# Attention in front of two mixture layers: rotation two pairs ahead, the first head rotated by VectorE, a half-width rotation table, another order at the last pair

## The chip, the core and the metric

One core of a Trainium2 chip runs one program: attention over 16 heads, then two mixture-of-experts layers. The metric is device time in microseconds (us) from start to end of the program; lower is better. The engines named below are TensorE (PE in the rows; its weight loads are PEld), VectorE (DVE), ScalarE (ACT), GpSimd (POOL) and SyncE (SP), which issues most of the DMAs. Each engine works through its own instructions in program order.

## The reference, cut to what matters

Only the attention is touched by the change. Its result, reshaped to `x`, feeds the two mixture layers.

```python
batch, n_heads, seq, head_dim = (2, 8, 576, 64)
def rotate(x):
    x1, x2 = (x[..., :half], x[..., half:])
    return np.concatenate([x1 * cos - x2 * sin, x1 * sin + x2 * cos], axis=-1)
q_rot, k_rot = (rotate(q), rotate(k))
scores = scale * np.matmul(q_rot, k_rot.transpose(0, 1, 3, 2))
scores = scores - np.max(scores, axis=-1, keepdims=True)
attn = np.exp(scores)
attn = attn / (np.sum(attn, axis=-1, keepdims=True) + 1e-09)
return np.matmul(attn, v).astype(np.float32)
...
x = np.ascontiguousarray(attn_out.transpose(0, 2, 1, 3)).reshape(B * S, H * D)
x = _moe_ref(x=x, **moe_kwargs)
return _moe2_ref(x=x, **moe2_kwargs)
```

## The kernel before, in words

`attention` works on 16 heads `g` (2 batches of 8), in 8 pairs `P`; the first head of a pair has `h = 0`, the second `h = 1`. All is in float32. The order of the work is written out by hand: for each head a list of calls with a number each (`at(t, f, ...)`) is sorted by the number and run. The integer part of a number is the tile of 128 score rows (five per head) beside which the call stands; `SC` holds the numbers of the calls that recur.

For a pair, `load_q` and `load_k` bring the raw heads to `rawq` and `rawk` (one buffer each). `rot` turns them: two products with the sine part of the table into `t2`, a product with the cosine part in place, and a sum into `t1` (`t1q`, `t1k`: two buffers each, one pair in each). `t1q` holds each value twice, side by side; the second copy is written by a second sum for pair 0, and by two small DMAs on SyncE's queue (one per head) for the others. From pair 1 on, all of `rot` is GpSimd's. `prepare(P + 1, n)`, called in the first head of pair P, rotates the next pair and then calls `preload`, which loads the raw data of the pair after that; SyncE issues all these DMAs in program order and waits where a buffer is still in use.

`tq(g)` transposes the rotated q and k of head `g` on TensorE (15 small matmuls against `ident`, 10 that read `t1q` and 5 that read `t1k`), and ScalarE and VectorE copy the result out to `qk`. It stands at 1.5 of the head before. `score(g, i)` multiplies a tile, VectorE takes the negative maximum (`negmax`), ScalarE the exponential with its row sum. `te` transposes the exponentials (one half is copied out by ScalarE, the other, `te_b`, by VectorE), and `pv` multiplies them with v one pair later. `rcp` (4.4 of the second head) inverts the row sums on VectorE, and GpSimd spreads the result over a tile `rcp`. `rbc` (0.5 of the next first head) transposes that tile on TensorE, and `norm` scales the output `xn`. `xsplit` writes `xn` as a rounded part `xH` (ScalarE) and a rest `xL` (GpSimd).

`warm(n)` issues n matmuls on a zero tile `wb` with no use of the result: 8 and 6 at the start, 3 behind the first `tq`, and 3 in each of the five steps of head 0.

Behind head 15 a last list (`g == NG`) finishes the last two pairs and begins the first mixture layer: `m1.step` with k = 0 (12 matmuls and two copies), then k = 1, and the rest in `m1.rest`. `m1.wconv(s, part)` splits a block of weights into a rounded part (ScalarE, or VectorE with `True` as last argument) and a rest (GpSimd, line 607). Everything behind that is not touched.

Of the kernel before, what the change touches and what calls it, by code (L numbers as in the profile page):

```python
# [1133 lines left out]

WC = dict(a=2.5, b=4.6, c=1.9, d=2.5)


def attention(tc, nc, ps, pss, lp, q, k, v, rope, ident, xH, xL, m1):
    with ExitStack() as st:
# [46 lines left out]
        def load_v(P):  # L1186
            t = vs[P % 2]
            for h in range(2):
# [35 lines left out]

        def rot(P, n, hs=(0, 1), e1=G, e2=G):
            x, tb = raw[n], tab[n]
# [11 lines left out]

            e1.tensor_tensor(t2[:, o, :, 0:32], x[:, o, :, 32:64], table(64, 96), op=OP.mult)
            e1.tensor_tensor(t2[:, o, :, 32:64], x[:, o, :, 0:32], table(96, 128), op=OP.mult)  # L1240
            e2.tensor_tensor(x[:, o], x[:, o], table(0, 64), op=OP.mult)  # L1241
            e2.tensor_tensor(t1, x[:, o], t2[:, o], op=OP.add)  # L1242
# [137 lines left out]
        for g in range(NG + 1):  # L1380
# [6 lines left out]
            if g < NG:  # L1387
                for i in range(5):
# [6 lines left out]
                    if g == 0:  # L1395
                        at(i + 0.4, warm, WARM[3])
# [22 lines left out]
            if m1 and g == NG - 1:  # L1419
                at(WC["a"], m1.wconv, 0, 0, True)  # L1420
                at(WC["b"], m1.wconv, 0, 1, True)
                at(4.5, m1.wload, 2)
            if g == NG:
                at(0.0, norm, P - 2, 1)
                at(0.0, xsplit, P - 2)
                at(0.1, rbc, P - 1)
                at(0.2, pv, P - 1, 0, 0, 5)
                at(0.3, norm, P - 1, 0)
                if m1:
                    at(0.4, m1.step)  # L1430
                    at(0.5, m1.wconv, 1, 0)
                at(0.6, pv, P - 1, 1, 0, 5)
                if m1:
                    at(0.7, m1.wconv, 1, 1)
                    at(0.7, m1.gate_w)
                    at(0.7, m1.wload, 3)
# [71 lines left out]
```

## Time and profile before

| | us |
|---|---|
| median of 3 runs | 1195.23 (1194.79 to 1198.83) |
| the profiled execution: its time | 1194.06 |
| the profiled execution: its span | 1192.1 |
| TensorE busy | 1129.7 (95% of the span) |
| VectorE, ScalarE, GpSimd busy | 769.9, 373.2, 448.4 |

The attention is the first 220 us or so of the span; the rest is the two mixture layers. The span is what the rows cover; the time is 2 us longer. Busy time of an engine is summed over its instructions; a row of the trace's timeline gives when an instruction or a merged run of like instructions began, how long it was busy, how many there were, and in brackets how long the engine had been idle before it and who released it.

### The profile page before, as it was taken

What the parts mean: (1) busy time and instruction counts of PE and PEld (TensorE: products, weight loads), DVE (VectorE), ACT (ScalarE), POOL (GpSimd) and SP (SyncE); (2) the same over time, 40 slices, a digit from 0 to 9 for tenths busy, and PEclk for the clock granted to TensorE, in tenths of its full rate; (3) what the DMA queues carried; (4) which work ended last, traced back from release to release, by engine and by line L of the source; (5) the groups of instructions that cost most, each with busy time, mean ns of one, the idle gap of its engine ahead of it and who ended that gap; (6) DMA issues with size and microseconds to landing.
All of it is one profiled execution on the core that took longest, in us unless ns stands there. A gap on an engine that the chain in (4) does not pass through costs nothing.

```text
span 1192.1 us, 20710 instructions
## 1 busy us (share of the span) xinstructions
PE 1129.7 (95%) x8147; PEld 975.2 (82%) x8147; DVE 769.9 (65%) x1721; ACT 373.2 (31%) x851; POOL 448.4 (38%) x432
## 2 busy tenths in 40 slices
PE   6877777999999999999999999999999999999997
PEld 3555545799888988888898888888989887899997
DVE  5655556146467777777777777666668888889200
ACT  3655555322332323232323232332232120222222
POOL 6345551521643544344434443544320000364121
PEclk7988888999999999999999999999999999999999
DMA  4121113310022232324222322121113003878830
GB/s 110 37 52 42 42 42 93 100 48 1 31 68 71 90 114 89 89 71 131 82 89 86 118 89 90 47 60 36 36 60 118 27 1 122 279 270 285 270 102 20
DMA packets 105297, 107.57 MB, mean 90 GB/s; under 512 B 35440, under 2 KB 68336, under 8 KB 105072
## 3 DMA queue, kind: packets, MB, share of 16 engines
q1 hardware_dynamic: 102864, 100.80, 27.1%
q0 software_dynamic: 2048, 4.72, 1.3%
q8 instruction: 64, 1.05, 0.4%
q10 hardware_dynamic: 288, 0.72, 0.2%
q14 instruction: 33, 0.27, 0.1%
HBM read 99.21 MB, written 4.72 MB: 87 GB/s over the span
## 4 chain that ended last, share of the span: by engine, by line
PE 81%; POOL 7%; issue 5%; DVE 3%; DMA 3%; ACT 1%; SPq 0%; POOLq 0%; DVEq 0%; ACTq 0%
PE Y L927 24%; PE T L865 22%; PE Y L701 8%; PE T L682 8%; PE Y L422 5%; PE Y L432 4%; PE PV L1319 2%; PE S L1283 1%; PE T L1260 1%; DMA t1q<-t1q 1%; POOL rawk L1241 1%; PE T L241 1%; POOL t1k L1242 1%; POOL rawq L1241 1%; POOL t1q L1242 1%
## 5 line engine op out<-in xcount | busy, mean ns | idle before, releaser
L929 DVE SCALAR_TENSOR_TENSOR acc<-Y,pw,acc 128x512 f32<-128x512 f32 x216 | 158.3, 743 | 1.5 <-PE Y L927 0.4
L865 PE MATMUL T<-xH,wa 128*128 128x256 f32 (+1 forms) x576 | 137.4, 294 | 0.8 <-ACT v L885 0.8
L865 PEld LDWEIGHTS T<-big,wb 128*128 128x128 f32 x864 | 125.8, 188 | 10.5 <-DVE v L878 1.4
L878 DVE TENSOR_TENSOR v<-T,v 128x256 f32<-128x256 f32 (+1 forms) x240 | 108.3, 451 | 38.2 <-PE T L865 35.3
L865 PE MATMUL T<-big,wb 128*128 128x256 f32 (+1 forms) x864 | 132.8, 296 | 0.0
L865 PEld LDWEIGHTS T<-xH,wa 128*128 128x128 f32 x576 | 100.0, 188 | 8.3 <-ACT v L885 2.5
L682 PE MATMUL T<-xH,wa 128*128 128x384 f32 x336 | 92.9, 337 | 0.0
L1285 DVE TENSOR_REDUCE negmax<-S 128x1 f32<-128x576 f32 (+1 forms) x80 | 60.2, 753 | 48.0 <-PE S L1283 47.9
L774 POOL TENSOR_TENSOR wa<-wraw,wa 128x512 fp32r<-128x512 f32 (+1 forms) x48 | 48.9, 1019 | 104.9 <-ACT wa L773 104.9
L865 PE MATMUL T<-xL,wa 128*128 128x256 f32 (+1 forms) x288 | 84.5, 293 | 0.0
L872 DVE SCALAR_TENSOR_TENSOR hlB<-v,hhB 128x320 fp32r<-128x320 f32 x72 | 56.9, 790 | 38.8 <-ACT hhB L871 38.8
L871 ACT ACTIVATE hhB<-v 128x320 fp32r<-128x320 f32 x72 | 34.0, 472 | 136.0 <-DVE v L878 136.0
L871 ACT ACTIVATE hhA<-v 128x256 fp32r<-128x256 f32 x72 | 30.1, 418 | 148.2 <-DVE v L878 148.2
L927 PE MATMUL Y<-wa,hhB 128*128 128x512 f32 x240 | 75.3, 396 | 0.0
L927 PE MATMUL Y<-wb,hhB 128*128 128x512 f32 x240 | 75.2, 395 | 0.0
L872 DVE SCALAR_TENSOR_TENSOR hlA<-v,hhA 128x256 fp32r<-128x256 f32 x72 | 50.6, 702 | 35.3 <-ACT hhA L871 35.3
L1000 DVE SCALAR_TENSOR_TENSOR fr<-fr,fc 128x512 f32<-128x512 f32 x64 | 52.5, 820 | 32.0 <-DMA fr<-in_moe_w 32.0
L793 POOL TENSOR_TENSOR wb<-wraw,wb 128x512 fp32r<-128x512 f32 x24 | 30.6, 1296 | 102.0 <-ACT wb L792 102.0
L701 PE MATMUL Y<-wb,hh 128*128 128x512 f32 x216 | 68.3, 397 | 0.0
L793 POOL TENSOR_TENSOR wa<-wraw,wa 128x512 fp32r<-128x512 f32 x24 | 30.6, 1292 | 99.8 <-ACT wa L792 99.8
L1283 PE MATMUL S<-qk 64*128 64x288 f32 x320 | 63.9, 477 | 1.5 <-ACT big L1288 1.4
L682 PEld LDWEIGHTS T<-xH,wa 128*128 128x128 f32 x336 | 61.3, 188 | 2.9 <-issue 0.9
(286 smaller groups left out, 2667.5 us busy)
## 6 DMA issues: line engine op xcount, KB each, us to landing
wraw<-in_moe_w SPq DMA_DIRECT2D x52, 512.0 KB, 5.4
fr<-in_moe_w SPq DMA_DIRECT2D x64, 256.0 KB, 4.2
wraw<-in_moe_w SPq DMA_DIRECT2D x48, 256.0 KB, 2.8
big<-in_moe_w SPq DMA_DIRECT2D x20, 512.0 KB, 4.6
wa<-in_moe_w SPq DMA_DIRECT2D x18, 512.0 KB, 3.9
wb<-in_moe_w SPq DMA_DIRECT2D x14, 512.0 KB, 4.2
fc<-in_moe_w_gate SPq DMA_DIRECT2D x9, 256.0 KB
ysc<-acc SPq DMA_DIRECT2D x9, 256.0 KB, 2.1
```

Of the source, the lines that this page charges most:

```text
L422: nc.tensor.matmul(Z["ph"][:, f % 2], d["wa"][kt // 2][:, kt % 2, f * 128:(f + 1) * 128], Z["xg", p][:, kt], start=(kt == 0), stop=(kt == ...
L682: nc.tensor.matmul(p[:, :CH], w[:, wi, kt, (fb % 2) * 128:(fb % 2) * 128 + 128], x[:, kt, o], start=(n == 0), stop=(n == 11))
L701: nc.tensor.matmul(self.Y[c][t], a[:, o], w[:, wi, fb % 2], start=(fb == 0 and n == 0), stop=(fb == FB - 1 and n == 2))
L793: G.tensor_tensor(d["W"][:, 1, h], r[:, 2 + h], d["W"][:, 0, h].bitcast(F32), op=OP.subtract)
L865: nc.tensor.matmul(bank[:, 0:n], d[t][:, ww, b, r * 128:(r + 1) * 128], x(xw, r), start=(first and i == 0), stop=(i == 5), skip_group_chec ...
L871: A.activation(HH[:, f, o], src, AF.Relu)
L872: V.scalar_tensor_tensor(HL[:, f, o], src, 0.0, HH[:, f, o].bitcast(F32), op0=OP.max, op1=OP.subtract)
L878: V.tensor_tensor(o, bank[:, 0:n], x, op=OP.add)
L927: nc.tensor.matmul(y, h[:, f, o], w[:, ww, f], start=(f == 0 and z == 0), stop=(f == 1 and z == 2))
L929: V.scalar_tensor_tensor(self.acc[:, t], y, self.pw[:, t, e:e + 1], self.acc[:, t], op0=OP.mult, op1=OP.add)
L1283: T.matmul(p[:, a, :288], QK[g][o, i * 128:(i + 1) * 128], QK[g][o, 640:928], start=True, stop=True)
L1285: V.tensor_reduce(m[0:n], p[0:n, :, :288], axis=AX.XY, op=OP.max, negate=True)
```

## The change

- Rotation two pairs ahead: `prepare(P + 2, ...)` stands in the second head of pair P, where `prepare(P + 1, ...)` stood in the first. So the raw data of pair P + 3 are loaded then. Pair 1 is prepared apart: its k on GpSimd before the loop, its q on VectorE in head 0, at 2.6 and 3.6.
- Pair 0: head 0 is rotated by VectorE as before, with the `wb` memset between k and q; the second copy of `t1q` is written by ScalarE. `tq(0)` follows at once, then head 1's k on VectorE (before: GpSimd) and its q on GpSimd.
- Table: the host sends 64 columns (cosine, sine) in place of 128; ScalarE writes the full table from them with six activations. The first q and its tail are issued on ScalarE's queue.
- `warm`: 6, 2, and 2 in each step of head 0, in place of 8, 6, 3 and 3.
- `xsplit`: the rounded part `xH` is GpSimd's but for the last pair. `rcp` of the last pair is spread by ScalarE.
- Last pair: the weight splits stand at 0.6, 1.6 and 3.6 of head 15 (before 2.5 and 4.6, and one behind it); `m1.step` with k = 0 stands ahead of `rbc` and `pv`, k = 1 between the two `pv`.

```diff
-WC = dict(a=2.5, b=4.6, c=1.9, d=2.5)
+WC = (0.6, 1.6, 3.6)
...
+        tcs = pone.tile([128, 11, 64], F32, name="tcs")
         load_k(nc.sync, 0, (0,), False)
-        A.dma_start(tab["k"], rope[:, 5:11])
-        load_q(nc.sync, 0, (0,), False)
-        A.dma_start(tab["q"], rope[:, 0:5])
+        A.dma_start(tcs[:, 5:11], rope[:, 5:11])
+        load_q(A, 0, (0,), False)
+        A.dma_start(tcs[:, 0:5], rope[:, 0:5])
...
+        for n, o in (("k", slice(5, 11)), ("q", slice(0, 5))):
+            A.activation(tab[n][:, :, 64:96], tcs[:, o, 32:64], AF.Copy, scale=-1.0)
+            A.activation(tab[n][:, :, 96:128], tcs[:, o, 32:64], AF.Copy)
+            A.activation(tab[n][:, :, 0:64].rearrange("p j (u c) -> p j u c", u=2),
+                         tcs[:, o, 0:32].unsqueeze(2).to_broadcast([128, SL[n], 2, 32]), AF.Copy)
...
             if U == 2:
-                dup = T1[n, P][:, o, :, 1]
-                if P == 0:
-                    e2.tensor_tensor(dup, x[:, o], t2[:, o], op=OP.add)
+                d = T1[n, P][:, o, :, 1]
+                if dup is None:
+                    for i in range(len(hs)):
+                        nc.sync.dma_start(d[:, i], t1[:, i])
                 else:
-                    for i in hs:
-                        nc.sync.dma_start(dup[:, i], t1[:, i])
+                    dup(d, t1)
...
-            A.activation(xH[:, pr, o], XN[P], AF.Copy)
+            if P < NP - 1:
+                G.tensor_copy(xH[:, pr, o], XN[P])
+            else:
+                A.activation(xH[:, pr, o], XN[P], AF.Copy)
...
+        def copy(d, x):
+            A.activation(d, x, AF.Copy)
+
+        rot(0, "k", (0,), V)
+        V.memset(wb, 0.0)
+        rot(0, "q", (0,), V, copy)
         warm(WARM[0])
-        rot(0, "k", (0,), V, V)
-        rot(0, "q", (0,), V, V)
-        warm(WARM[1])
-        rot(0, "k", (1,), G, G)
-        rot(0, "q", (1,), G, G)
+        tq(0)
+        rot(0, "k", (1,), V)
+        rot(0, "q", (1,), G, copy)
         preload(1, "k")
         preload(1, "q")
-        tq(0)
-        warm(WARM[2])
+        warm(WARM[1])
+        rot(1, "k")
+        preload(2, "k")
...
-                if h == 0:
-                    at(SC["rk"], prepare, P + 1, "k")
-                    at(SC["rq"], prepare, P + 1, "q")
-                else:
+                if g == 0:
+                    at(2.6, rot, 1, "q", (0,), V)
+                    at(3.6, rot, 1, "q", (1,), V)
+                    at(3.6, preload, 2, "q")
+                if h == 1:
+                    at(SC["rk"], prepare, P + 2, "k")
+                    at(SC["rq"], prepare, P + 2, "q")
                     at(SC["rcp"], rcp, P)
...
-                at(WC["a"], m1.wconv, 0, 0, True)
-                at(WC["b"], m1.wconv, 0, 1, True)
-                at(4.5, m1.wload, 2)
+                for t, w in enumerate(((0, 0, True), (0, 1, True), (1, 0))):
+                    at(WC[t], m1.wconv, *w)
+                at(1.6, m1.wload, 2)
...
-WARM = (8, 6, 3, 3)
+WARM = (6, 2, 2)
```

Three places show what the new order does. The first is GpSimd's list from the rotation of pair 1 to the first spread of inverted sums (`rcp`). Before, pair 1's k and q (`t1k_244`, `t1q_323`) stand ahead of it, and pair 2's begin behind it:

```order
L1239 TENSOR_TENSOR t2k_244<-rawk_96,tabk_98 128x12x32
L1240 TENSOR_TENSOR t2k_244<-rawk_96,tabk_98 128x12x32
L1241 TENSOR_TENSOR rawk_96<-rawk_96,tabk_98 128x768
L1242 TENSOR_TENSOR t1k_243<-rawk_96,t2k_244 128x768
L1239 TENSOR_TENSOR t2q_324<-rawq_95,tabq_97 128x10x32
L1240 TENSOR_TENSOR t2q_324<-rawq_95,tabq_97 128x10x32
L1241 TENSOR_TENSOR rawq_95<-rawq_95,tabq_97 128x640
L1242 TENSOR_TENSOR t1q_323<-rawq_95,t2q_324 128x10x64
L1327 COPY rcp_492<-den_489 128x640
L1239 TENSOR_TENSOR t2k_531<-rawk_96,tabk_98 128x12x32
```

Of the change, the end of pair 1's k (`t1k_203`), then all of pair 2 (`t1k_392`, `t1q_464`), the same `rcp`, and pair 3's k behind it:

```order
L1247 TENSOR_TENSOR t1k_203<-rawk_96,t2k_204 128x768
L1244 TENSOR_TENSOR t2k_393<-rawk_96,tabk_98 128x12x32
L1245 TENSOR_TENSOR t2k_393<-rawk_96,tabk_98 128x12x32
L1246 TENSOR_TENSOR rawk_96<-rawk_96,tabk_98 128x768
L1247 TENSOR_TENSOR t1k_392<-rawk_96,t2k_393 128x768
L1244 TENSOR_TENSOR t2q_465<-rawq_95,tabq_97 128x10x32
L1245 TENSOR_TENSOR t2q_465<-rawq_95,tabq_97 128x10x32
L1246 TENSOR_TENSOR rawq_95<-rawq_95,tabq_97 128x640
L1247 TENSOR_TENSOR t1q_464<-rawq_95,t2q_465 128x10x64
L1334 COPY rcp_511<-den_508 128x640
L1244 TENSOR_TENSOR t2k_677<-rawk_96,tabk_98 128x12x32
```

So the `rcp` of pair P, which stood behind the rotation of pair P + 1, stands behind that of pair P + 2.

The second place is VectorE's opening, of the change, from the last memset to the second rotation of k (the same list before has the `wb` memset ahead of the first row, a second sum of line 1246 ahead of the `qk` copy, and `negmax` right behind that copy):

```order
L1216 MEMSET big_100 128x64 x3
L1244 TENSOR_TENSOR t2k<-rawk,tabk 128x6x32
L1245 TENSOR_TENSOR t2k<-rawk,tabk 128x6x32
L1246 TENSOR_TENSOR rawk<-rawk,tabk 128x384
L1247 TENSOR_TENSOR t1k<-rawk,t2k 128x384
L1382 MEMSET wb 128x256
L1244 TENSOR_TENSOR t2q<-rawq,tabq 128x5x32
L1245 TENSOR_TENSOR t2q<-rawq,tabq 128x5x32
L1246 TENSOR_TENSOR rawq<-rawq,tabq 128x320
L1247 TENSOR_TENSOR t1q<-rawq,t2q 128x5x64
L1278 COPY qk<-T 128x7x64
L1244 TENSOR_TENSOR t2k<-rawk,tabk 128x6x32
```

The last row is the first of four that rotate k of head 1; they have come between the copy of head 0's transposes and its first maximum.

The third place is ScalarE's list from head 15's end to the second step of the mixture layer. Before, with `hh` of `m1.step` k = 0 and k = 1 behind the copies `rs` of `rbc`:

```order
L1336 ACTIVATE rs_2566<-T_2567 128x4x64
L1338 ACTIVATE rs_2566<-T_2567 128x64
L690 ACTIVATE hh_2611<-T_2598 128x384
L606 ACTIVATE wa_2615<-wraw_2406 128x1024
L606 ACTIVATE wb_2629<-wraw_2406 128x1024
L538 ACTIVATE gg_2409<-g1_2404 128x4x8
L1349 ACTIVATE xH_71<-xn_2592 128x576
L690 ACTIVATE hh_2653<-T_2640 128x384
```

And of the change:

```order
L606 ACTIVATE wa_2543<-wraw_2402 128x1024
L1336 ACTIVATE rcp_2556<-den_2553 128x640
L690 ACTIVATE hh_2582<-T_2569 128x384
L606 ACTIVATE wb_2586<-wraw_2402 128x1024
L1345 ACTIVATE rs_2589<-T_2590 128x4x64
L1347 ACTIVATE rs_2589<-T_2590 128x64
L690 ACTIVATE hh_2630<-T_2617 128x384
L538 ACTIVATE gg_2405<-g1_2400 128x4x8
```

The first `hh` and both weight splits now stand ahead of `rs`, and `rcp` is in this list.

## Rows read from the trace of the kernel before

**Rows 1.** Page, span in 40 equal slices: granted clock in tenths.

```profile
PEclk7988888999999999999999999999999999999999
```

**Rows 2.** Waits, 0 to 240 us: total us, times, longest.

```profile
PE T L1260 <- DMA t1q<-t1q: 30.1, 6, 5.5
```

**Rows 3.** Timeline of TensorE: transposes of rotated q that begin `tq`.

```profile
32.90 0.53 PE L1260 MATMUL T<-ident,t1q 64*128 64x64 f32 x9 [0.50 <-ACT pt L1306]
...
41.16 0.52 PE L1260 MATMUL T<-ident,t1q 64*128 64x64 f32 x9 [0.47 <-ACT pt L1306]
...
52.34 0.53 PE L1260 MATMUL T<-ident,t1q 64*128 64x64 f32 x10 [2.71 <-DMA t1q<-t1q]
...
63.51 0.85 PE L1260 MATMUL T<-ident,t1q 64*128 64x64 f32 x10 [0.27 <-ACT rs L1338]
...
77.79 0.80 PE L1260 MATMUL T<-ident,t1q 64*128 64x64 f32 x10 [5.47 <-DMA t1q<-t1q]
...
193.80 0.85 PE L1260 MATMUL T<-ident,t1q 64*128 64x64 f32 x10 [0.27 <-ACT rs L1338]
```

**Rows 4.** Windows: busy us by engine, then granted clock, DMA share, GB/s.

```profile
82.80:84.10 1.30, 1.30 (x8) 0.57 (x6) 0.00 (x0) 0.00 (x0) 0.00 (x0) 0.60 0.00 0
...
88.00:114.00 26.00, 19.76 (x220) 13.38 (x222) 14.55 (x30) 13.98 (x35) 12.37 (x10) 0.87 0.23 53
```

**Rows 5.** Timeline of GpSimd and SyncE's queue, pair 2 to 3.

```profile
63.14 1.41 POOL L1350 TENSOR_TENSOR xL<-xn,xH 128x576 fp32r<-128x576 f32 x1 [1.89 <-ACT xH L1349]
...
64.51 1.00 POOL L1239 TENSOR_TENSOR t2k<-rawk,tabk 128x384 f32<-128x384 f32 x1
...
73.58 1.53 POOL L1242 TENSOR_TENSOR t1q<-rawq,t2q 128x640 f32<-128x640 f32 x1
...
75.14 1.33 SPq L1249 DMA_DIRECT2D t1q<-t1q  x2
...
87.12 0.72 POOL L1327 COPY rcp<-den 128x640 f32<-128x640 f32 x1 [12.01 <-DVE den L1325]
```

**Rows 6.** Lines by shape, 30 to 200 us: busy, mean ns, idle before.

```profile
L1306 ACT ACTIVATE pt<-T 128x320 f32<-128x320 f32 x56 | 24.4, 436 | 42.5 <-PE T L1260 42.5
...
L1349 ACT ACTIVATE xH<-xn 128x576 fp32r<-128x576 f32 x6 | 4.0, 673 | 0.0
```

**Rows 7.** Timeline of the opening: VectorE and TensorE.

```profile
6.79 0.36 DVE L1239 TENSOR_TENSOR t2k<-rawk,tabk 128x192 f32<-128x192 f32 x1 [5.14 <-DMA rawk<-in_k]
...
8.79 0.70 DVE L1239 TENSOR_TENSOR t2q<-rawq,tabq 128x160 f32<-128x160 f32 x1
...
12.45 0.80 DVE L1246 TENSOR_TENSOR t1q<-rawq,t2q 128x320 f32<-128x320 f32 x1
...
13.40 0.80 PE L1260 MATMUL T<-ident,t1q 64*128 64x64 f32 x10 [6.84 <-DVE t1q L1246]
...
17.18 0.76 DVE L1285 TENSOR_REDUCE negmax<-S 128x1 f32<-128x576 f32 x1 [2.11 <-PE S L1283]
```

**Rows 8.** Timeline of the opening: SyncE's queue and GpSimd, pair 1.

```profile
9.78 2.58 SPq L1175 DMA_DIRECT2D rawk<-in_k  x4
...
15.69 0.99 POOL L1239 TENSOR_TENSOR t2k<-rawk,tabk 128x384 f32<-128x384 f32 x1
...
21.34 0.86 POOL L1239 TENSOR_TENSOR t2q<-rawq,tabq 128x320 f32<-128x320 f32 x1
```

**Rows 9.** Timeline at the last pair: VectorE and TensorE.

```profile
205.00 0.68 DVE L604 CAST wa<-wraw 128x1024 fp32r<-128x1024 f32 x1
...
209.62 0.52 PE L1260 MATMUL T<-ident,rcp 64*128 64x64 f32 x9 [2.01 <-POOL rcp L1327]
```

**Rows 10.** Chain that ended last, at the last pair: start, us, what.

```profile
210.14 4.26 PE PV L1319 x20
...
216.68 2.58 PE PV L1319 x20
...
223.59 2.08 PE T L682 x12
```

More of the change, by code (lines that the diff above doesn't have):

```diff
@@ L1204, in attention @@
         load_k(nc.sync, 0, ())
-        load_q(nc.sync, 0, ())
+        load_q(A, 0, ())
         load_k(nc.sync, 0, (1,), False)
@@ L1213, in attention @@
         wb = one.tile([128, 512], BF, name="wb")
-        V.memset(wb, 0.0)
         for i in range(NE):
             V.memset(eb[i][:, 576:640], 0.0)
+        for n, o in (("k", slice(5, 11)), ("q", slice(0, 5))):
[3 more added lines that the diff above has]
+                         tcs[:, o, 0:32].unsqueeze(2).to_broadcast([128, SL[n], 2, 32]), AF.Copy)
         def warm(n):
@@ L1223, in attention, with rot @@
         T1 = {}
-        def rot(P, n, hs=(0, 1), e1=G, e2=G):
+        def rot(P, n, hs=(0, 1), e=G, dup=None):
             x, tb = raw[n], tab[n]
@@ L1237, in table @@
                 return tb[:, :, lo:hi].unsqueeze(1).to_broadcast([128, len(hs), J, hi - lo])
[L1239 to L1242, printed above, removed]
+            e.tensor_tensor(t2[:, o, :, 0:32], x[:, o, :, 32:64], table(64, 96), op=OP.mult)
+            e.tensor_tensor(t2[:, o, :, 32:64], x[:, o, :, 0:32], table(96, 128), op=OP.mult)
+            e.tensor_tensor(x[:, o], x[:, o], table(0, 64), op=OP.mult)
+            e.tensor_tensor(t1, x[:, o], t2[:, o], op=OP.add)
             if U == 2:
-                dup = T1[n, P][:, o, :, 1]
-                if P == 0:
-                    e2.tensor_tensor(dup, x[:, o], t2[:, o], op=OP.add)
-                else:
-                    for i in hs:
-                        nc.sync.dma_start(dup[:, i], t1[:, i])
+                d = T1[n, P][:, o, :, 1]
+                if dup is None:
+                    for i in range(len(hs)):
+                        nc.sync.dma_start(d[:, i], t1[:, i])
+                else:
+                    dup(d, t1)
         QK, EB, PT, PV, RS, XN = {}, {}, {}, {}, {}, {}
@@ L1326, in rcp @@
             r = RS["d", P] = two.tile([128, 5, 2, HD], F32, name="rcp")
-            G.tensor_copy(r, d.rearrange("p h j -> p j h").unsqueeze(3).to_broadcast([128, 5, 2, HD]))
+            x = d.rearrange("p h j -> p j h").unsqueeze(3).to_broadcast([128, 5, 2, HD])
+            if P < NP - 1:
+                G.tensor_copy(r, x)
+            else:
+                A.activation(r, x, AF.Copy)
         def rbc(P):
@@ L1348, in xsplit @@
             o = slice(b * S, (b + 1) * S)
-            A.activation(xH[:, pr, o], XN[P], AF.Copy)
+            if P < NP - 1:
+                G.tensor_copy(xH[:, pr, o], XN[P])
+            else:
+                A.activation(xH[:, pr, o], XN[P], AF.Copy)
             G.tensor_tensor(xL[:, pr, o], XN[P], xH[:, pr, o].bitcast(F32), op=OP.subtract)
@@ L1395, in attention @@
                     if g == 0:
-                        at(i + 0.4, warm, WARM[3])
+                        at(i + 0.4, warm, WARM[2])
                 if g + 1 < NG:
                     at(SC["tq"], tq, g + 1)
-                if h == 0:
-                    at(SC["rk"], prepare, P + 1, "k")
-                    at(SC["rq"], prepare, P + 1, "q")
-                else:
+                if g == 0:
[5 more added lines that the diff above has]
+                    at(SC["rq"], prepare, P + 2, "q")
                     at(SC["rcp"], rcp, P)
@@ L1425, in attention @@
                 at(0.0, xsplit, P - 2)
-                at(0.1, rbc, P - 1)
+                if m1:
+                    at(0.1, m1.step)
+                    at(0.1, m1.wconv, 1, 1)
+                at(0.2, rbc, P - 1)
                 at(0.2, pv, P - 1, 0, 0, 5)
@@ L1430, in attention @@
                     at(0.4, m1.step)
-                    at(0.5, m1.wconv, 1, 0)
+                    at(0.4, m1.gate_w)
+                    at(0.4, m1.wload, 3)
                 at(0.6, pv, P - 1, 1, 0, 5)
[L1433 to L1436, printed above, removed]
                 at(0.8, norm, P - 1, 1)
-                if m1:
-                    at(0.9, m1.step)
                 at(0.85, xsplit, P - 1)
@@ L1456, in host_consts @@
     tok = token_order()
-    rope = np.zeros((128, 11, 128), np.float32)
+    rope = np.zeros((128, 11, 64), np.float32)
     rows = [(np.float32(0.125), tok[j * 128:j * 128 + 128]) for j in range(5)]
@@ L1463, in host_consts @@
         rope[:n, j, 0:32] = cos[s] * sc
-        rope[:n, j, 32:64] = cos[s] * sc
-        rope[:n, j, 64:96] = -sin[s] * sc
-        rope[:n, j, 96:128] = sin[s] * sc
+        rope[:n, j, 32:64] = sin[s] * sc
     rt = np.zeros((128, 328), np.float32)
```

## The prediction

> **What bounds it now.** I read the page first. Its clock slices show where time lies: the granted clock is full (2.4 GHz) from slice 9 on and lower in the first seven slices, about 209 us, which are the attention [rows 1]. Since all else is untouched and TensorE runs through it without a break, I read only the attention, and ask when TensorE gets from one `tq` to the next.
>
> The list of waits names one large wait of TensorE there: its transposes of rotated q wait for the DMA that doubles `t1q`, 30.1 us in six waits [rows 2]. The timeline shows where: at the `tq` of each even head. That of head 4 waits 2.71 us, that of head 6 5.47 us [rows 3], and those of heads 8 to 14 as long: 2.71 and five times 5.47 make the 30.1. What is late is seen on GpSimd: the rotation of the next pair begins at 64.51, after `xL`, and its last sum, which began at 73.58, ends at 75.11; SyncE issues the doubling at 75.14, and the transposes begin at 77.79 [rows 3, 5]. So a chain of 10.6 us of rotation and 2.7 us of DMA begins where the pair before it is under way, and TensorE is done with what it has at 72.32, that is 5.47 before 77.79.
>
> The wait has a second price. Behind it the granted clock is at its half level (1.2 GHz); the window from 82.80 to 84.10, 5 us after that `tq`, still shows 0.60 [rows 4].
>
> Now the two halves of a pair. From the odd head's `tq` to the even one's it is 14.28 (63.51 to 77.79), the wait included, so 8.81 of work at full clock. From head 4 to head 15 it is 141.46 (52.34 to 193.80) [rows 3]: five such halves (71.40), and six of the other kind, from even to odd, with 70.06, or 11.68 each. These hold the same five tiles, 20 `pv` matmuls and one `tq`, plus `rbc`, whose transposes are 0.52 at full clock [rows 9]. So at full clock one should take 8.81 + 0.5 = 9.3; the 2.4 between that and 11.68 I put down to the half level, and a stretch of some 5 us at half clock, as the window shows, would give just that.
>
> The other engines have room: in the window from 88 to 114, one pair, VectorE has 14.55 us of work, ScalarE 13.98, GpSimd 12.37 [rows 4]. A pair without wait and at full clock would be 8.81 + 9.3 = 18.1.
>
> **The change, part by part.**
>
> *Rotation two pairs ahead.* The rotated pair and its doubling are now ready a whole pair, about 18 us, before their `tq`. The wait goes: 5 × 5.47 = 27.4 us from head 6 on (head 4 comes with the opening). With it goes the half clock, 6 × 2.4 = 14.3; bounds 0, if other waits keep the clock down, and 6 × (11.68 − 8.81) = 17.2. What is late next is `rcp`, which stands behind the rotation on GpSimd. The two `t1` buffers let a rotation write once the odd head's `tq` has read; that is at the same place at which `xL` ends now. So it still begins about 1 us after an odd `tq` and ends 11.6 after it (63.51 to 75.11). The `den` that releases `rcp` came at 87.12, 9.33 after the even `tq` at 77.79 [rows 3, 5]; less 2.4 to 2.9 of half clock this is about 6.6, so 8.81 + 6.6 = 15.4 after the odd one. GpSimd is free 3.8 us before. Also moved: six loads of raw k, three of q and two doublings per pair on SyncE's queue. They wait for the rotation as before, in the same order, and have a pair's time; v's loads stand behind them and wait for `pv` anyway. I put these at nothing; uncovered, a doubling costs 2.7.
>
> *`xH` on GpSimd.* ScalarE's is 0.673 [rows 6]. GpSimd's cast isn't in the trace; the nearest rows are the spread of `rcp`, 640 columns in 0.72, and `xL`, 576 columns with two inputs in 1.41 [rows 5]. I take 0.65, being nearer to the first; at 1.41 the 3.8 us margin covers it. It takes the place of a wait of GpSimd for ScalarE (1.89, which is most of the way to `xL`). On ScalarE it frees the copies `rs`, on which the odd `tq` waits 0.27 [rows 3]: 6 × 0.27 = 1.6, bounds 0 and 6 × 0.673 = 4.0.
>
> *Opening.* Head 0's k takes 2.0 on VectorE (6.79 to 8.79), its q 3.66 (8.79 to 12.45) beside GpSimd, and the second sum 0.80 [rows 7]. Now `wb` stands between (a quarter us, my estimate), and ScalarE's copy, for which the row of 128x320 gives 0.436 [rows 6], replaces the 0.80. The smaller table and q's loads on another queue may let k begin up to 1 us earlier; ScalarE's six copies of the table (0.3 to 0.5 each by the same row) hide behind k's landing, but cost up to 1 if not. I take 0 for these. `tq(0)` moves from 13.40 to 13.2. Head 1's k (2.0) now runs ahead of the first maximum, which was 3.78 behind `tq(0)` with three filler matmuls in between; I put it at 17.0 instead of 17.18. In head 0 five filler batches lose one matmul each, about 1.5 us together; VectorE gets eight products and sums, 2 × 2.0 to 2 × 3.66, of which I count 2.5 on the path, the rest in its gaps. So `tq(2)` comes at about 33.7 instead of 32.90.
>
> GpSimd is late here. SyncE's loads of pair 1's k began at 9.78 and the rotation at 15.69, 5.9 later, with waits between the loads [rows 8]. Without them I take 4.4 (an estimate). The loads now wait for head 1's k on VectorE, done at about 16; two of the six need not. So the rotation of pair 1's k runs from about 20 to 25.8 (12 of 22 column blocks of a pair's 10.6). Then pair 2's k is loaded: rotation from 30.2, 10.6 long, to 40.8, and only then `rcp` of pair 0 (0.71), done at 41.5. Before, it was done at 39.12 and `tq(3)` came at 41.16, 2.04 behind it [rows 3, 8]; so `tq(3)` moves to 43.5. `tq(4)` needs no wait: 52.34 − 41.16 − 2.71 = 8.47 after that, 52.0. The opening gains 0.4; bounds −3 and +3.
>
> On this the Trainium skill speaks against the change. VectorE's q took 3.66 beside GpSimd where k, with more columns, took 2.0 alone [rows 7]; that is the row. "SBUF — State Buffer", section "SBUF: two separate sides", says that an op of VectorE with two SBUF inputs and a GpSimd op exclude each other for a whole instruction, the loser waiting. By it each of the eight new VectorE ops could wait out one GpSimd op; with 1.00 to 1.53 per op [rows 5] that is up to 10 us where I counted 2.5, and a sum 7 us worse, my upper bound. It holds only where both rotate at once, and by the times above GpSimd waits for data in much of head 0.
>
> *Last pair.* The step k = 0 of the mixture layer fills the wait of 2.01 for `rcp` [rows 9], and the `pv` behind it runs at full clock: 20 matmuls took 4.26 there and 2.58 later [rows 10]. That is 2.01 + 1.68 = 3.7. Against it, the weight casts of VectorE, 0.68 each [rows 9], now stand among head 15's tiles; one was among them before, so 0.7. Net 3.0, bounds 1.3 and 3.7. It counts up to 223.59, where the third step begins; from there all follows TensorE.
>
> **Sum.** 27.4 + 14.3 + 1.6 + 0.4 + 3.0 = 46.7. The profiled execution took 1194.06 (span 1192.1), so 1147.4; the median shown is 1.2 above it: **1148.5 us**.
>
> **Rivals.**
> - *Another engine bounds the pair.* VectorE's 14.55 and ScalarE's 13.98 would fill 80% of an 18.1 us pair, and tile by tile they hand work to each other. If a pair takes 20.3 for it, this gives back 6 × 2.2: 1162. For it: the density. Against it: the half of 8.81 ran with GpSimd rotating beside it, and TensorE had no gap there.
> - *The wait moves to `rcp`.* If GpSimd's rotation takes over 14.4 instead of 10.6, `rbc` waits in each pair. At 2.5 us with the half clock again (2.4), 6 × 4.9: 1178. For it: it happens once in the opening by my sum. Against it: the 3.8 us margin.
> - *Slower.* GpSimd has 12.37 of work per pair, 13 with `xH`; if the denser VectorE work doubled that, GpSimd would bound the pair at 26.3, today's length, and from there on every us costs six. At 2.2 times, 28.6, it ends at about 1206. The rows show no such slowing in the loop.
> - *No effect.* The doubling stays late because of SyncE's order: 1195. Its queue has a full pair of slack against it.
>
> **Chances.** The sum (1141 to 1156) 0.72; the engine bound 0.13; `rcp` 0.08; slower 0.03; no effect 0.02; better than 1141, should ScalarE's relief be worth its upper bound and the clock rise early in the opening, 0.02. The likeliest one's own bounds are the opening's ±3, 2.9 more of clock or some of it missing, and 1.7 at the end. The range 1141 to 1164 takes in the engine-bound case. Anything under 6 us (0.5%) could not be told from no change: faster 0.95, same 0.02, slower 0.03.
>
> **What would show it.** Right: no wait for `t1q`'s DMA in the list; `tq` to `tq` about 8.8 and 9.1 in turn; clock slices of 9 from the third or so; one wait for `rcp` near 41 us; the first step of the mixture layer ahead of `rbc`. Wrong: halves above 10 at full clock with TensorE waiting for copies; `rcp` as releaser in every pair; an opening whose `tq(4)` comes behind 55.

## The result and the profile after

The changed kernel takes 1163.81 us (median of 4 runs, 1159.14 to 1165.00) against 1196.45 (4 runs, 1194.79 to 1198.83): ratio 0.9718, 95% interval 0.9684 to 0.9753. The time lies in the predicted range, but 0.2 us below its upper end (1164), with two of the four runs above it, and 15.3 us above the value; of a gain forecast at 46.7 us, 32.6 came. The profiled execution took 1162.72, its span is 1160.8.

The page of the changed kernel, engines' busy time and granted clock by slices:

```profile
PE 1117.1 (96%) x8133; PEld 969.4 (84%) x8133; DVE 776.6 (67%) x1732; ACT 373.0 (32%) x853; POOL 443.1 (38%) x429
...
PEclk9799999999999999999999999999999999999999
```

Against [rows 1] the low slices are gone but for the second, about 29 to 58 us. The list of waits has no entry for the DMA that doubles `t1q` any more, where [rows 2] had 30.1 us. What TensorE waits for in the attention now, 0 to 215 us (total us, times, longest):

```profile
...
PE T L1265 <- ACT pt L1311: 6.8, 14, 0.5
PE S L1288 <- ACT big L1293: 4.7, 5, 1.7
PE T L1265 <- POOL rcp L1334: 3.3, 7, 1.8
PE T L1265 <- ACT qk L1277: 2.0, 6, 0.3
...
PE T L1265 <- ACT rs L1347: 1.7, 6, 0.3
```

TensorE's timeline, with the rows that answer to [rows 3], one pair's waits in between (112.63 to 132.41), and the last pair. Where one transpose stands apart ahead of a wait for `pt`, the time of `tq` is that of the row behind the wait:

```profile
26.72 0.76 PE L1288 MATMUL S<-qk 64*128 64x288 f32 x4 [1.69 <-ACT big L1293]
...
31.69 0.79 PE L1265 MATMUL T<-ident,t1q 64*128 64x64 f32 x9 [0.42 <-ACT pt L1311]
...
40.02 0.79 PE L1265 MATMUL T<-ident,rcp 64*128 64x64 f32 x9 [1.79 <-POOL rcp L1334]
...
42.94 0.79 PE L1265 MATMUL T<-ident,t1q 64*128 64x64 f32 x9 [0.42 <-ACT pt L1311]
...
53.32 0.46 PE L1265 MATMUL T<-ident,t1q 64*128 64x64 f32 x8 [0.53 <-ACT pt L1311]
...
112.63 0.52 PE L1265 MATMUL T<-ident,t1q 64*128 64x64 f32 x9 [0.52 <-ACT pt L1311]
...
114.22 0.52 PE L1265 MATMUL T<-ident,big 64*128 64x64 f32 x9 [0.34 <-ACT qk L1277]
...
120.53 0.74 PE L1265 MATMUL T<-ident,rcp 64*128 64x64 f32 x9 [0.24 <-POOL rcp L1334]
...
122.16 0.52 PE L1265 MATMUL T<-ident,big 64*128 64x64 f32 x9 [0.29 <-ACT rs L1347]
...
123.15 0.46 PE L1265 MATMUL T<-ident,t1q 64*128 64x64 f32 x8 [0.47 <-ACT pt L1311]
...
132.41 0.28 PE L1265 MATMUL T<-ident,t1q 64*128 64x64 f32 x2 [0.52 <-ACT pt L1311]
...
162.70 0.52 PE L1265 MATMUL T<-ident,t1q 64*128 64x64 f32 x9 [0.47 <-ACT pt L1311]
...
176.69 0.52 PE L1265 MATMUL T<-ident,big 64*128 64x64 f32 x5 [1.94 <-ACT big L1293]
...
178.26 0.45 PE L682 MATMUL T<-xH,wa 128*128 128x384 f32 x1
...
180.55 0.52 PE L1265 MATMUL T<-ident,rcp 64*128 64x64 f32 x9
181.00 2.65 PE L1324 MATMUL PV<-pt,big 128*64 128x288 f32 x20
...
190.49 0.45 PE L682 MATMUL T<-xH,wa 128*128 128x384 f32 x1
```

A pair is 19.78 us (112.63 to 132.41), 10.52 from the even to the odd `tq` and 9.26 back. Both halves end in a wait of half a microsecond for `pt`, ScalarE's copy that empties the bank `tq` needs; the longer one also has waits for `qk`, `rcp` and `rs`. Windows of the changed kernel (us, busy us by engine and instructions, granted clock, DMA share, GB/s), two in the opening and the two halves before and after 112.63:

```profile
core 0: us, PE busy (x) PEld busy (x) DVE busy (x) ACT busy (x) POOL busy (x), PEclk, DMA share, GB/s
30.00:40.00 10.00, 7.54 (x80) 5.97 (x76) 7.33 (x13) 5.72 (x16) 9.34 (x9) 0.67 0.24 58
40.00:46.00 6.00, 5.56 (x54) 4.47 (x56) 3.27 (x7) 3.41 (x10) 5.58 (x5) 0.50 0.42 105
103.38:112.63 9.25, 8.61 (x100) 5.71 (x100) 6.05 (x12) 6.11 (x15) 9.02 (x8) 1.00 0.12 27
112.63:123.15 10.52, 9.18 (x109) 5.97 (x110) 7.99 (x17) 6.72 (x18) 4.05 (x5) 1.00 0.40 95
```

At full clock, then, no engine is filled: TensorE is busy 17.79 of 19.77 us, VectorE 14.0, ScalarE 12.8, GpSimd 13.1.

**Where the gain of the attention comes from.** The third step of the mixture layer begins at 190.49, before at 223.43 by the timeline (the chain of [rows 10] has 223.59): 32.9 less. Up to `tq(4)` the change loses 1.0 (53.32 against 52.34). From there to `tq(15)` it gains 32.1 (109.38 against 141.46): 25.1 in the five halves from odd to even (46.3 against 71.40), 7.0 in the six from even to odd (63.1 against 70.06). Behind `tq(15)` it gains 1.8 (27.79 against 29.63). Behind the attention nothing is changed, yet from the first matmul of the gate to the end two executions took 965.2 and 971.2 us (e6 and e9 below); so kernels are compared below by times inside the attention, and the whole time only where it was measured in rounds.

Three rows of the opening and three of the last pair on VectorE and GpSimd; beside [rows 7, 9] they are the ones that came out otherwise:

```profile
21.97 1.94 POOL L1247 TENSOR_TENSOR t1k<-rawk,t2k 128x768 f32<-128x768 f32 x1
22.16 1.93 DVE L1245 TENSOR_TENSOR t2q<-rawq,tabq 128x160 f32<-128x160 f32 x1
...
25.06 0.75 DVE L1290 TENSOR_REDUCE negmax<-S 128x1 f32<-128x576 f32 x1
...
172.20 2.36 POOL L607 TENSOR_TENSOR wa<-wraw,wa 128x1024 fp32r<-128x1024 f32 x1 [8.88 <-DVE wa L604]
173.05 2.06 DVE L604 CAST wb<-wraw 128x1024 fp32r<-128x1024 f32 x1
...
180.33 0.67 POOL L1359 CAST xH<-xn 128x576 fp32r<-128x576 f32 x1
```

### The profile page after: what moved, and what is told of

The parts are those of the page before. It is cut to its first block, busy times and chain, and to the rows that moved or that the text cites. A ratio compares the mean times of both kernels' runs of the same rounds, so it can differ in the third digit from the quotient of the medians.

```text
span 1160.8 us, 20699 instructions
## 1 busy us (share of the span) xinstructions
PE 1117.1 (96%) x8133; PEld 969.4 (84%) x8133; DVE 776.6 (67%) x1732; ACT 373.0 (32%) x853; POOL 443.1 (38%) x429
## 5 line engine op out<-in xcount | busy, mean ns | idle before, releaser
L865 PEld LDWEIGHTS T<-xH,wa 128*128 128x128 f32 x576 | 100.0, 188 | 8.7 <-ACT v L885 3.0
L871 ACT ACTIVATE hhA<-v 128x256 fp32r<-128x256 f32 x72 | 30.1, 418 | 148.4 <-DVE v L878 148.4
L1293 ACT ACTIVATE big<-S,negmax 128x576 f32<-128x576 f32 (+1 forms) x80 | 59.1, 738 | 19.2 <-DVE negmax L1290 15.6
```

What stands on the lines that cost most here:

```text
L865: nc.tensor.matmul(bank[:, 0:n], d[t][:, ww, b, r * 128:(r + 1) * 128], x(xw, r), start=(first and i == 0), stop=(i == 5), skip_group_chec ...
L871: A.activation(HH[:, f, o], src, AF.Relu)
L1293: pexp.append(lambda: A.activation(e[0:n, :576].rearrange("p (a c) -> p a c", a=2), p[0:n, :, :288], AF.Exp, bias=m[0:n], scale=1.0, accum ...
```

## The experiments

Theory after the result: the missing gain is not a new long wait. A half without the long wait is longer than the 8.81 that was left beside it, because short waits for copies, which lay inside the long one, come out; and taking the half clock away gave back less than was put down to it. In the opening VectorE's new rotations hold up the maxima. Rivals: another engine's busy time sets the pair; GpSimd's list and `rcp` are what is late.

All kernels by TensorE's timeline (`tq` of head 4 and 15, a pair as a fifth of head 4 to head 14, and the start of the mixture layer's third step). In e5, e9, e10 and e12 twelve `pv` matmuls, 1.7 us, stand ahead of `tq` and not behind it, so their `tq` times are not to be held against the others'; pairs and the third step are:

| kernel | tq(4) | tq(15) | pair | third step | median us (runs) |
|---|---|---|---|---|---|
| before | 52.34 | 193.80 | 26.07 | 223.43 | 1196.45 (4) |
| changed | 53.32 | 162.70 | 19.77 | 190.49 | 1163.81 (4) |
| e1_xh_act | 51.90 | 160.69 | 19.74 | 188.89 | 1158.97 (1) |
| e2_pv_spread | 53.70 | 172.05 | 21.53 | 199.06 | 1173.81 (4) |
| e3_half_max | 53.45 | 158.10 | 18.95 | 185.30 | 1157.81 (1) |
| e4_ahead_alone | 49.71 | 158.22 | 19.68 | 186.25 | 1161.01 (4) |
| e5_pv_cover | 53.03 | 160.46 | 19.45 | 187.06 | 1158.70 (1) |
| e6_q_pool | 53.34 | 162.75 | 19.78 | 190.55 | 1159.73 (1) |
| e7_kq_pool | 49.09 | 158.45 | 19.77 | 186.25 | 1158.37 (1) |
| e8_one_ahead | 51.16 | 192.96 | 26.06 | 222.31 | 1192.51 (1) |
| e9_pool_order | 51.45 | 159.26 | 19.52 | 187.43 | 1156.58 (6) |
| e10_pool_order_rcp | 48.82 | 156.60 | 19.52 | 183.22 | 1154.22 (5) |
| e11_no_accum | 53.36 | 161.80 | 19.60 | 191.07 | 1165.94 (1) |
| e12_relief | 54.27 | 157.07 | 18.61 | 182.90 | 1155.23 (1) |

**Which part makes the gain: e4_ahead_alone and e8_one_ahead.** The first is the kernel before with the rotation two pairs ahead and nothing else:

```diff
-                if h == 0:
-                    at(SC["rk"], prepare, P + 1, "k")
-                    at(SC["rq"], prepare, P + 1, "q")
-                else:
+                if g == 0:
+                    at(SC["rk"], prepare, 1, "k")
+                    at(SC["rq"], prepare, 1, "q")
+                if h == 1:
+                    at(SC["rk"], prepare, P + 2, "k")
+                    at(SC["rq"], prepare, P + 2, "q")
```

> The kernel before with the rotation two pairs ahead alone: opening, table, filler matmuls, xH and last pair as before; pair 1 is rotated by GpSimd in head 0 as before. If the removed DMA wait is nearly all of the gain: tq of head 4 to that of head 15 takes 109 to 112 us (changed kernel 109.4, before 141.5) and the time is 1160 to 1167, as fast as the changed kernel. If the other parts carry it: above 1172.

It took 1161.01 (1156.07 to 1163.48), ratio 0.9720 (0.9675 to 0.9765): as fast as the whole change. From `tq(4)` to `tq(15)` it took 108.5. Its pair is the same within 0.1, its `tq(4)` 3.6 us earlier, and its last pair, in the old order, at full clock too:

```profile
174.12 0.52 PE L1260 MATMUL T<-ident,rcp 64*128 64x64 f32 x9 [2.10 <-POOL rcp L1327]
174.57 2.65 PE L1319 MATMUL PV<-pt,big 128*64 128x288 f32 x20
```

From `tq(15)` to the third step it took 28.03 (158.22 to 186.25), the changed kernel 27.79: the wait of 2.10 for `rcp` is still there, and the new order at the last pair is worth 0.2, not 3.0; 1.6 of the 1.8 gained there is the clock of `pv` (2.65 against 4.26 in [rows 10]).

The second is the changed kernel with `prepare(P + 1, ...)` in the first head again, from pair 2 on:

```diff
+                if h == 0 and P > 0:
+                    at(SC["rk"], prepare, P + 1, "k")
+                    at(SC["rq"], prepare, P + 1, "q")
                 if h == 1:
-                    at(SC["rk"], prepare, P + 2, "k")
-                    at(SC["rq"], prepare, P + 2, "q")
```

> The changed kernel with the rotation back at one pair ahead, in the first head, from pair 2 on; all other parts stay. Theory (the rotation two pairs ahead is the whole gain): the wait for the doubling of t1q is back at 5 to 5.5 us in each pair, the pair at 26 to 26.5, and the time at 1190 to 1198. Rival (the copy xH that left ScalarE, and ScalarE's relief, have a part): the pair at 25.5 or less, the time below 1188.

Its list of waits, 0 to 240 us, has the old entry back; the pair is 26.06 and the time that of before, 1192.51 where before took 1192.92:

```profile
PE T L1265 <- DMA t1q<-t1q: 29.6, 6, 5.4
```

So the rotation two pairs ahead is both enough and needed; all other parts together bring nothing that the times show. In the traces they rather cost: e4 reaches the third step 4.2 us before the changed kernel.

**`xH` on ScalarE again: e1_xh_act.** Both branches of `xsplit` write `xH` by `A.activation`.

> The changed kernel with the rounded part xH back on ScalarE in all pairs. A pair of heads (tq of head 6 to tq of head 8) takes 19.77 us in the changed kernel. The prediction's term (0.27 per pair, at most 0.673): 20.0 to 20.4 here. If ScalarE has room at that place and the cast merely moved: 19.8, no difference.

The pair is 19.74 against 19.77. The wait for `rs` stays: 0.27 at the odd `tq` in e1, 0.29 one run of transposes earlier in the changed kernel (122.16). The term of 1.6 us was nothing, and the expectation of a longer pair falls too.

**What sets the pair at full clock: e2, e3, e5, e11, e12.**

```diff
-                    at(SC["pva"], pv, P - 1, h, 0, 3)
-                    at(SC["pvb"], pv, P - 1, h, 3, 5)
+                    for t in range(5):
+                        at((0.6, 1.6, 2.5, 3.5, 4.5)[t], pv, P - 1, h, t, t + 1)
```

> The changed kernel with the pv matmuls of a head given out one column block per tile (4 matmuls at each of five tiles) in place of 12 and 8. Hand-off theory: TensorE idles 2.0 us of 19.8 per pair since the tiles without pv are paced by ScalarE's and VectorE's copies while the tiles with pv leave those engines idle; spread, a pair should take 17.9 to 18.6 and the program 7 to 11 us less than the changed kernel. Rival, the idle time is a fixed cost of handing over at each tile, or the wait of tq for banks: 19.5 to 20 and no difference in time.

It was slower than the changed kernel: 1173.81, ratio to before 0.9829 (0.9774 to 0.9883). It brought a wait of its own, so it does not tell the theories apart. `pv` has one bank; spread over the head it gives the bank back at the head's end, and `pv` then stands for `norm` to empty it, 1.48 us in one head of a pair and 0.28 in the other (e2's timeline of TensorE):

```profile
94.55 0.71 PE L1324 MATMUL PV<-pt,big 128*64 128x288 f32 x4 [1.48 <-DVE xn L1353]
```

For e5 one number is changed: `pva` from 2.5 to 1.4, so three tiles of `pv` stand ahead of `tq`.

> The changed kernel with one number changed: the first three tiles of pv stand ahead of tq in each head instead of behind it, so that 1.6 us of matmuls lie between the transposes of e and those of tq, which now wait 0.5 us for ScalarE's copy pt. Theory (the missing gain is TensorE's short waits for copies, and they are a matter of order): the waits at tq vanish and a pair falls from 19.8 to 18.6 to 19.0 us, the end 4 to 6 us earlier. Rival (VectorE's and ScalarE's chain from tile to tile sets the pace, whatever TensorE does in between): the pair stays at 19.6 to 19.9, and the half microsecond comes up at the next transposes, for qk or for big. A wait of pv for xn, as in the run with pv spread, would make it longer than 19.8.

The half microsecond at `tq` goes, but the pair only falls to 19.45. The waits of TensorE in one pair of e5, 72.47 to 91.92 us, are these (the changed kernel has 1.0 for `pt` and 0.3, 0.3 and 0.2 for `qk`, `rs` and `rcp`):

```profile
PE S L1288 <- ACT big L1293: 0.4, 2, 0.2
PE PV L1324 <- DVE xn L1353: 0.3, 1, 0.3
PE T L1265 <- ACT rs L1347: 0.3, 1, 0.3
PE T L1265 <- ACT pt L1311: 0.2, 1, 0.2
```

Of 1.8 us in a pair 0.6 went; what was `pt` is now partly `big`, the exponential. So the order gave a third of the microsecond looked for, and the rival, the chain from tile to tile, held the rest. For e3 the maximum takes half the columns, `p[0:n, :, :144]`; for e11 the exponential writes no row sums (no `accum_out`); e12 has both and e5's order.

> The changed kernel with the maximum taken over half of the columns of each tile (left out: the other half; a maximum over fewer columns is only another shift of the exponent). VectorE's op per tile falls from 0.75 to about 0.45, 3 us per pair. If VectorE is what the tiles without pv wait for, a pair falls from 19.77 to 18.2 to 18.9; if it is ScalarE alone, to no less than 19.4.

> The changed kernel with the exponential not summed along its row, so that ScalarE's 0.19 us read of the accumulator falls away in each tile (the sums stay at one, so the output is not normalised). 10 tiles of a pair: 1.9 us of ScalarE's 13. Theory (a tile passes from TensorE to VectorE's maximum, to ScalarE's exponential and back, and that chain sets the pair, as the halved maximum showed with 0.82 less): the pair at 18.8 to 19.5. Rival (VectorE alone sets it): 19.7 to 19.8. If TensorE alone set it: no change either.

> The changed kernel with the maximum over half the columns, without the sums, and with pv ahead of tq: all three reliefs at once (the output is not the attention's). TensorE's work of a pair is 17.8 to 18.0 us. Theory (TensorE's missing time are its waits in the chain from tile to tile): the pair at 18.0 to 18.6, with TensorE busy over 96% of it. Rival (something further bounds it): 18.7 to 19.0, no less than with the halved maximum alone, 18.95.

Halving VectorE's maximum (455 ns against 753, 3.0 us in a pair) takes 0.82 off the pair, ScalarE's accumulator read (1.9 us in a pair) 0.17, all three 1.16. The three pairs, 18.95, 19.60 and 18.61, each came just above the range expected of it. In e12 TensorE is then busy 95% of the pair:

```profile
72.88:91.49 18.61, 17.73 (x211) 11.58 (x209) 11.41 (x27) 11.53 (x22) 13.07 (x12) 1.00 0.29 68
```

No engine's busy time is the bound, since 3.0 us of VectorE gave 0.82; nor is TensorE's alone. A tile goes from TensorE's `S` to VectorE's maximum, to ScalarE's exponential and back to TensorE's transposes, two tiles ahead, and each end of a link that comes late is a short wait of TensorE. In e3 the list of a pair (72.40 to 91.34) has `pt` alone, 1.5 us in three waits; those for `qk`, `rs` and `rcp` are gone. The chain fits e3, e5, e11 and e12, but it is not shown link by link. Single values here come from one execution each; pairs of one trace agree within 0.3 us.

**The opening: e6, e7, e9, e10.** In e6 pair 1's q is GpSimd's; in e7 head 1's k too:

```diff
-        rot(0, "k", (1,), V)
+        rot(0, "k", (1,), G)
...
-                    at(2.6, rot, 1, "q", (0,), V)
-                    at(3.6, rot, 1, "q", (1,), V)
-                    at(3.6, preload, 2, "q")
+                    at(2.6, prepare, 1, "q")
```

> The changed kernel with pair 1's q rotated by GpSimd in head 0, where VectorE does it now. In the changed kernel VectorE's ops of it took up to 1.93 us beside GpSimd's, negmax came late at 25 us, and tq of head 4 came at 53.3 us; with rotation two pairs ahead alone it came at 49.7. Theory (VectorE is held up by GpSimd's ops, and the first maxima with it): tq(4) at 50.5 to 51.5. Rival (the 4.8 us of q on GpSimd push the first rcp back, from 39 to 44 us): the wait for rcp grows and tq(4) comes at 55 to 58. If neither matters, since the half clock sets the opening, tq(4) stays within 0.7 of 53.3. From there to tq(15) all three say 109.4.

`tq(4)` came at 53.34, unmoved, but for none of the three reasons. The maxima now came on time, and a wait took the place of theirs, for the doubling of pair 1's q. The rows are of e6's TensorE and GpSimd:

```profile
19.12 0.99 POOL L1244 TENSOR_TENSOR t2k<-rawk,tabk 128x384 f32<-128x384 f32 x1 [8.83 <-DMA rawk<-in_k]
...
32.43 0.79 PE L1265 MATMUL T<-ident,t1q 64*128 64x64 f32 x10 [4.93 <-DMA t1q<-t1q]
```

GpSimd's rotation of pair 1 waits for raw k, whose buffer comes free when VectorE has rotated head 1's k; in e6 that ended at 15.21, and GpSimd stood idle 8.83 us.

> As the run before, and head 1's k on GpSimd too, so that VectorE rotates head 0 alone, as in the kernel before; the smaller table, the early tq(0) and the filler counts stay. Theory (VectorE's rotations cost the opening its gain): tq(4) at 47.5 to 49.5, since tq(0) keeps the 2.4 us by which it is earlier than with rotation two pairs ahead alone (11.4 against 13.8), where tq(4) came at 49.7. Rival (GpSimd's list is what is late): 50 to 54, with a wait for rcp of 2 us or more ahead of tq(3).

It came at 49.09, 4.2 us before the changed kernel's, and the third step 4.2 us earlier too. The same rows of e7, with its wait for `rcp`:

```profile
13.95 0.99 POOL L1244 TENSOR_TENSOR t2k<-rawk,tabk 128x384 f32<-128x384 f32 x1 [0.17 <-DMA rawk<-in_k]
...
27.26 0.79 PE L1265 MATMUL T<-ident,t1q 64*128 64x64 f32 x10 [0.51 <-DMA t1q<-t1q]
...
35.95 0.80 PE L1265 MATMUL T<-ident,rcp 64*128 64x64 f32 x9 [3.16 <-POOL rcp L1334]
```

So head 1's k on VectorE costs most: it keeps GpSimd from starting, and pair 1's q then has to come from somewhere. e9 joins e7 and e5; e10 also puts pair 2's q behind `rcp` of pair 0:

```diff
-                    at(SC["rq"], prepare, P + 2, "q")
+                    at(SC["rq"] if P else 4.6, prepare, P + 2, "q")
```

> The changed kernel with head 1's k and pair 1's q on GpSimd and with pv ahead of tq in each head, so the two runs that each gave something, together. If the two add up: tq of head 4 at 49.1 instead of 53.3 (4.2 us), a pair of 19.44 instead of 19.77 (5.5 pairs, 1.8 us), so 5 to 7 us below the changed kernel: 1156 to 1159 as a median, ratio 0.967 to 0.971. Rival: what starts earlier only waits longer for rcp of pair 0 (3.2 us in the run with both on GpSimd): 2 to 4 us below.

> As the run before, and in pair 0 alone the rotation of pair 2's q stands behind rcp on GpSimd, not ahead of it. Theory (in the opening, rcp of pair 0 is late because it stands behind the rotation of pair 2, and TensorE waits 3.2 us for it and then runs at half clock): the wait falls below 1 us, tq(4) comes at 44 to 47, the end 3 to 5 us before the run before. Rival (something else ends there at the same time, as den of VectorE or the doubling of pair 2): less than 1 us.

e9 took 1156.58 (1153.46 to 1162.75), ratio 0.9683 (0.9658 to 0.9707), as the first expectation said in the median. Its profiled execution, the longest of the six, does not show the two parts adding up: its third step comes 3.1 us before the changed kernel's, where e7 gained 4.2 and e5 3.4. e10 took 1154.22 (1151.66 to 1157.69), ratio 0.9655 (0.9634 to 0.9677), so its interval overlaps that of e9. The wait for `rcp` fell from 2.70 to 0.99 and the clock held, but `tq(4)` came at 48.82, not 44 to 47. The rows are of TensorE in e9, then of GpSimd and TensorE in e10:

```profile
36.44 0.79 PE L1265 MATMUL T<-ident,rcp 64*128 64x64 f32 x9 [2.70 <-POOL rcp L1334]
```

```profile
35.74 0.71 POOL L1334 COPY rcp<-den 128x640 f32<-128x640 f32 x1 [5.77 <-DVE den L1330]
...
36.51 0.52 PE L1265 MATMUL T<-ident,rcp 64*128 64x64 f32 x9 [0.99 <-POOL rcp L1334]
```

The new order is not shown to be the cause. `rcp` began at 35.67 in e9, behind GpSimd's list, and at 35.74 in e10, now behind VectorE's `den`, as the rival had it; TensorE's transposes of it stand at the same place in both. The wait is shorter because TensorE came to it 1.8 us later. It was that much later at `tq(1)` already, 21.89 against 20.11, and the lists are the same up to there: this much of the opening is not the code's. e10's windows, to be held against the changed kernel's:

```profile
30.00:40.00 10.00, 8.37 (x114) 5.89 (x116) 7.42 (x16) 7.45 (x20) 4.10 (x5) 1.00 0.14 33
40.00:46.00 6.00, 5.72 (x72) 3.90 (x69) 4.45 (x8) 3.86 (x10) 5.84 (x5) 1.00 0.41 104
```

e10 has the lowest median of the study, 9.6 us below the changed kernel's, with intervals of the ratios that do not meet; by the third step it is 7.3 us ahead.

## Why the prediction was right, and where it was off

The mechanism of the main term was right, and the time fell into the range by a hair. 1163.81 is not in the 1141 to 1156 that the sum was given with a chance of 0.72; it is in the part that was added to the range for the engine-bound rival (1162, chance 0.13). For the sum that is luck: the pair came near that rival's length, and not for its cause. One of the signs set down for being wrong came too: halves above 10 at full clock with TensorE waiting for copies.

**The removed wait: right.** 27.4 was forecast and 25.1 came. The 2.3 between them is the first thing missed: with the doubling early, the odd-to-even half is 9.26, not 8.81, since it ends in a wait of 0.52 for `pt` (132.41) that had been spent inside the 5.47. In the loop no engine waits for a DMA or load moved to SyncE's later place. TensorE waits 0.24 for `rcp` in each pair; GpSimd is free 5.2 us before `den` releases it, where 3.8 was forecast.

**The clock: the step that was mis-sized.** "So at full clock one should take 8.81 + 0.5 = 9.3; the 2.4 between that and 11.68 I put down to the half level." At clock 1.00 this half takes 10.52, and the term of 14.3 was 7.0. Windows of the kernel before, first the half of 8.81 with its wait of 5.47, then three of the six halves from even to odd:

```profile
63.51:77.79 14.28, 8.63 (x100) 5.65 (x101) 6.86 (x13) 7.26 (x18) 11.29 (x9) 0.97 0.18 43
77.79:90.08 12.29, 11.71 (x109) 7.58 (x109) 6.97 (x15) 6.14 (x16) 1.07 (x2) 0.75 0.22 53
104.36:115.39 11.03, 10.45 (x110) 7.18 (x110) 6.99 (x15) 6.14 (x16) 1.08 (x2) 0.85 0.25 59
129.67:141.68 12.01, 11.42 (x110) 7.45 (x110) 6.99 (x15) 6.15 (x16) 1.08 (x2) 0.78 0.23 54
```

The price of the half level, 2.4 for some 5 us, was about right. A granted clock of 0.75 over 12.29 us is 6.1 us at the half level (2 × 0.25 × 12.29); 0.85 is 3.3 us and 0.78 is 5.3. TensorE's busy time in these halves is 2.5, 1.3 and 2.2 above the 9.18 at full clock, 0.38 to 0.42 for each of these us. From the shortest of the three to the others, one more us at the half level makes the half 0.45 and 0.49 longer.

Wrong was the length at full clock. TensorE idles 0.18 in the half of 8.81 (14.28 − 5.47 − 8.63) and 0.58 in each of the other three, whatever their clock. In the changed kernel it idles 1.34 (10.52 − 9.18), in the waits for `qk`, `rcp`, `rs` and `pt`. The 9.3 of the forecast held 0.2 of this, with the work for `rbc` rightly sized (0.5, measured 0.57). So most of the missing 1.2 of a half is short waits. A pair says the same: 18.1 was forecast, TensorE's busy time is 17.79, and the 1.7 up to 19.77 is waiting that the sum had put at nothing.

How the gain divides between this term and the wait's hangs on where `tq` is counted. In e4, which has the lists of before apart from the rotation, the halves are 10.10 and 9.58, so that the two terms are 9.5 and 23.5 in place of 7.0 and 25.1. Not shown is why the short waits are fewer in the kernel before: slower matmuls may fill them, or the other engines catch up during the long wait.

The rival "another engine bounds the pair" was nearest in its number, 20.3 for 19.77, and in its "tile by tile they hand work to each other", but not in its name, as e3, e11 and e12 show. What I held against it, that the half of 8.81 had no gap, was wrong: its gap lay in the wait.

**`xH`: 1.6 forecast, nothing came** (e1). GpSimd's cast took 0.67 (0.65 taken); ScalarE's relief took no wait away.

**Opening: 0.4 gain forecast, 1.0 lost.** `tq(0)` came at 11.39 (13.2), `tq(2)` at 31.69 (33.7), `tq(3)` at 42.94 (43.5): GpSimd's list and the late `rcp` were foreseen, though what released `rcp` was VectorE's `den`, 0.34 after GpSimd was free. Of the 2.0 us ahead at `tq(2)` 0.6 was left at `tq(3)`; from there to `tq(4)` it took 10.38 where I took 8.47 from before: TensorE ran at 0.50 from 40 to 46 us, after its waits of 1.69 at 26.72, 1.52 at 29.31 and 1.79 at 40.02. In e10 the clock was 1.00 there and that stretch 9.26. The loss of 1.0 is within what one list varies by: e1, whose lists are the changed kernel's up to there, reached `tq(4)` at 51.90, which is the 0.4 that was forecast. Not weighed was that the raw buffer ties GpSimd's start to VectorE (e6, e7). The end of `rcp` at 39.12 in the prediction is the start and length of this row of GpSimd's timeline of before:

```profile
38.41 0.71 POOL L1327 COPY rcp<-den 128x640 f32<-128x640 f32 x1 [12.15 <-DVE den L1325]
```

**Last pair: 3.0 forecast, 1.8 came**, and 1.6 of it by the clock that the rotation gave back (e4). The step k = 0 does fill the wait for `rcp` (no wait at 180.55), but VectorE's cast, taken at 0.68, took 2.06, the maximum and the exponential of head 15's last tile came behind it, and TensorE waited 1.94 at 176.69 instead.

**VectorE beside GpSimd.** The Trainium skill's "SBUF — State Buffer", section "SBUF: two separate sides", has a VectorE op and a GpSimd op that want the shared port exclude each other for the whole op. The traces agree in kind: 1.93 for an op that took 0.31 alone, beside GpSimd's 1.94 (21.97 to 23.91), and the cast's 2.06 against 0.68, beside GpSimd's 2.36. The bound of 10 us was far off: of the twelve rotation ops that VectorE got anew one was held up, by 1.6 us. But ten of them ran while GpSimd had no op under way (10.39 to 18.04 and 23.91 to 28.30), so how often ops that do meet are held up is not shown. The prediction's "alone" for head 0's k is not exact: in the kernel before GpSimd's first rotation op began at 7.47, beside the second half of it. Head 1's k, with GpSimd idle, took 1.80 (12.98 to 14.78).

**Still open:** by how much the one held-up op and by how much the lost clock made the opening longer; taking either away alone was not tried.

## What to carry to other kernels

The stretch next to a long wait is no measure of the loop without that wait: short waits for copies hide inside it, and they come back once it is gone. Price a low clock by the busy time that it adds, from equal stretches at different granted clocks, and look for the waits at full clock apart from it: what the clock gives back in work can go into waiting. Before work goes to an engine with idle time in an opening, look at what that work releases (here a raw buffer and through it another engine's start).

## What was not expected of the hardware

Full clock gave back less than it saved in work: from the kernel before to the changed one TensorE's busy time in a half from even to odd fell by 1.9 us in the mean (11.09 to 9.17), the half itself by 1.2 (11.68 to 10.52). VectorE's `den`, an op on ten columns that takes 0.16 in the median, took 1.15 us once in the changed kernel's opening, beside GpSimd's sum of pair 2's q (37.36 to 38.90), and the first `rcp` waited for it.
